# Sliding-window attention with a SwiGLU block: one attention unit takes another place in the source, and some VectorE additions lose their priority

## The chip, the cores and the metric

The kernel runs on 1 core of one Trainium2 chip. The metric is the device time of one execution in microseconds (us). The time before is 343.68 us, the median of 3 runs (343.43 to 343.70).

## The reference

Attention with 8 batches, 8 heads, 576 positions and a head size of 64 is followed by a gated feed-forward block on the 4608 resulting rows of 512 numbers.

```python
scores = scale * np.matmul(q, k.transpose(0, 1, 3, 2))
mask = (rel >= 0) & (rel < 128)                 # rel = query position - key position
scores = np.where(mask, scores - slopes * np.abs(rel), -1e9)
attn = softmax(scores)                           # over the keys
x = np.matmul(attn, v)                           # heads side by side: 4608 x 512
g = x @ w_gate                                   # 512 x 1536
out = (g * sigmoid(g) * (x @ w_val)) @ w_out     # 1536 x 512
```

## The kernel before, in words

**Units and blocks.** Two batches make a group, `s`, of 1152 rows: four tiles of 128 rows from the first batch, four from the second, and one tile that combines the last 64 rows of both. These nine tiles are units `(s, p)`, `p` from 0 to 8, numbered 0 to 35. Unit 8 is the first combined one. The feed-forward part works in 9 blocks of 512 rows. Block 0 takes units 0 to 3, block 1 takes units 4 to 7, and so on; block 8 takes the four combined units. So unit 7 is the last of the four that block 1 needs.

**What a unit does.** TensorE transposes the keys and queries of the first ranks (`transposed`, L218); from rank 11 on a DMA on the sync queue does it (L239). `scores` makes the products of queries and keys in PSUM (`ps`, L278; or `psc`, L313, for tiles with only 128 queries), ScalarE takes the exponential (L284, L317), and VectorE multiplies with a mask (`ex`, L290; `exc`, L321). Unit 8 has three such `exc` tiles of 128x1024 elements, unit 7 has one. `weighted` (L325) makes the attention-value products on TensorE (`av`, L345), and VectorE divides them by the row sum in two halves (reciprocal L347, `x` L348). `x_transposed` (L358) transposes `x` on TensorE (`px`, L371), and ScalarE copies it into `xT` (L375).

**What a block does.** For blocks 0 to 5, each of 12 column groups has a gate product `pg` and a value product `pv` on TensorE, four matmuls of 512 columns each (L397). ScalarE makes a tanh of the gate (L415), VectorE multiplies it with the gate (`uu`, L416) and then with the value product (`hT`, L427). `pg` and `pv` share three PSUM banks (tag `gv`), so a product waits for VectorE to have read the one three before it. Scores, `av`, `px` and transposed tiles share four other banks (tag `a`). Blocks 6 to 8 compute gate and value with Strassen-Winograd's seven products of half size (`gate_val_by_seven`, L612). There a unit of two column groups holds the banks X, Y and Z (`gX`, `gY`, `gZ`); `third` adds Y and a saved sum into `v1` (L661), `seventh` adds X and a saved product into `v2` (L669), and `fourth` then writes X anew (L624), which must wait until that addition has read it. The output projection is `project` for block 0 (`po`, L451) and a seven-product form for all others (`strassen`, L504, products L532); its sums S2, S3 and S4 of the activations are made on VectorE (L485 to L488), and its results leave PSUM through `half_plus` (L535), among others.

**What sets the order.** GpSimd issues its loads in an order written out by hand. TensorE, VectorE and ScalarE keep the order of the source in the first part (up to 8 steps of the feed-forward part). After that a scheduler orders each engine's instructions: of those that it believes ready it takes the one that stands first in the source, and `tc.high_priority()` moves an instruction ahead. From step 60 (block 2) TensorE again keeps the order of the source, and VectorE and ScalarE stay with the scheduler. Before step 60 the scheduler also draws work forward as filler, so the projection of block 0 (`po`, L451) runs between the steps of units 7 and 8. The source interleaves the two parts: `everything` (L939) goes through the steps of `ffn` and after each one takes as many steps of the generator `attention` (L840) as a target says; it counts them in `n_att`. In `attention`, the turn of unit `i` emits the transpositions and scores of unit `i + 1`, then `weighted(i)`, then loads (`loads_to`, `ahead`), then `x_transposed(i)`; from unit 13 on the order differs a little (`late`).

The functions of the change:

Of the kernel before, what the change touches and what calls it, by code (L numbers as in the profile page):

```python
# [31 lines left out]
SEVEN_FROM = 6  # L32
# [19 lines left out]
def kernel(  # L52
# [10 lines left out]
    nc = tc.nc  # L63
# [440 lines left out]
    def strassen(n, t):  # L504

        h = hT[n]
        A11, A12 = h[:, 0:HM, 0:256], h[:, HM:NMB, 0:256]
        S1, A22 = h[:, 0:HM, 256:512], h[:, HM:NMB, 256:512]
        S2, S3, S4 = hsum[n]
        cols = slice(t * P, (t + 1) * P)  # L510
        end = n == NBLK - 1
        seeded = SEVEN_FROM <= n + 1 < NBLK
        factor = 1.0 if n >= SEVEN_FROM else 0.5
        if end:
            X, Y = (ps_a.tile([P, HC], FP32, name="po", tag="a", bufs=4) for _ in range(2))
            p2 = ps_f.tile([P, HC], FP32, name="p2", tag="gv")
        else:
            po = ps_f.tile([P, 2, HC], FP32, name="po", tag="po", bufs=1)
            X, Y = po[:, 0, :], po[:, 1, :]
            p2 = (ps_f.tile([P, HC], FP32, name="p2", tag="gv") if seeded  # L520
                  else ps_a.tile([P, HC], FP32, name="p2", tag="a"))
        top, low = (opool.tile([P, DM], FP32, name="osb", tag="osb") for _ in range(2))
        if end and t:
            spare = [opool.tile([P, DM], FP32, name="osb", tag="osb") for _ in range(2)]
            p1s, p5s, u2s = spare[0][:, 0:HC], spare[0][:, HC:DM], spare[1][:, 0:HC]
        else:
            p1s, p5s, u2s = (supool.tile([P, HC], FP32, name=i, tag=i, bufs=1)
                             for i in ("p1s", "p5s", "u2s"))

        def product(dst, a, b, start=False):  # L530
            for m in range(HM):
                nc.tensor.matmul(dst, a[:, m, cols], b[:, m, :], start=(start and m == 0),  # L532
                                 stop=(m == HM - 1), skip_group_check=True)

        def half_plus(dst, a, b):  # L535
            with tc.high_priority():
                nc.vector.scalar_tensor_tensor(out=dst, in0=a, scalar=factor, in1=b,
                                               op0=ALU.mult, op1=ALU.add)

        product(X, A11, B11, True)  # L540
        if seeded:
            nc.scalar.copy(p2, X)
        else:
            nc.scalar.mul(p1s, X, factor)
        yield
        product(p2, A12, B21, not seeded)
        if seeded:
            nc.vector.tensor_scalar_mul(top[:, 0:HC], p2, factor)
        else:
            half_plus(top[:, 0:HC], p2, p1s)  # L550
        if end and t:
            store(n, t, top, 0, HC)
        yield
        product(X, S2, T2)
        nc.scalar.mul(u2s, X, factor)
        yield
        product(Y, S1, T1, end)
        if end and t:
            nc.vector.tensor_scalar_mul(p5s, Y, factor)
        else:  # L560
            nc.scalar.mul(p5s, Y, factor)
        yield
        product(X, S3, T3)
        half_plus(low[:, HC:DM], X, p5s)
        if end and t:
            store(n, t + 2, low, HC, DM, True)
        yield
        product(Y, S4, B22)
        half_plus(top[:, HC:DM], Y, u2s)
        store(n, t, top, HC if end and t else 0, DM, end)  # L570
        yield
        product(X, A22, T4)
        if end:
            nc.vector.tensor_scalar_mul(low[:, 0:HC], X, factor)
        else:
            nc.scalar.mul(low[:, 0:HC], X, factor)
        store(n, t + 2, low, 0, HC if end and t else DM, end)
        yield
# [33 lines left out]
    def gate_val_by_seven(n):  # L612

        x = xT[n]
        A11, A12 = x[:, 0:HK, 0:256], x[:, HK:NKB, 0:256]
        S1, A22 = x[:, 0:HK, 256:512], x[:, HK:NKB, 256:512]
        S2, S3, S4 = xsum.pop(n)
        hT[n] = hpool.tile([P, NMB, 512], FP16, name="hT", tag="hT")
        live = {}

        def product(dst, w, c0, a, start=False):
            for i in range(2):
                for kb in range(HK):
                    nc.tensor.matmul(dst[:, i, :], w[:, kb, c0 + i * P:c0 + (i + 1) * P], a[:, kb, :],  # L624
                                     start=(start and i == 0 and kb == 0),
                                     stop=(i == 1 and kb == HK - 1), skip_group_check=True)

        def first(u):
            X, Y = (ps_a.tile([P, 2, 256], FP32, name=i, tag="a", bufs=4) for i in ("gX", "gY"))
            Z = ps_f.tile([P, 2, 256], FP32, name="gZ", tag="gv")  # L630
            live[u] = X, Y, Z
            product(X, G1, 2 * u * P, A11, True)
            nc.scalar.copy(Z, X)

        def fifth(u):
            Y = live[u][1]
            product(Y, tsum[u][0], 0, S1, True)
            p5 = epool.tile([P, 2, 256], FP32, name="p5", tag="exc", bufs=5)
            nc.scalar.copy(p5, Y)
            live[u] += (p5,)  # L640

        def second(u):
            Z = live[u][2]
            product(Z, G2, 2 * u * P, A12)
            s = supool.tile([P, 2, 256], FP16, name="s1", tag="tt")
            nc.scalar.activation(s, Z, AF.Silu)
            live[u] += (s,)

        def sixth(u):
            X = live[u][0]  # L650
            product(X, tsum[u][1], 0, S2)
            u2 = epool.tile([P, 2, 256], FP32, name="u2", tag="exc", bufs=5)
            nc.scalar.copy(u2, X)
            live[u] += (u2,)

        def third(u):
            X, Y, Z, p5, u2, s = live[u][:6]
            product(Y, V2, 2 * u * P, S4)
            v_ = supool.tile([P, 2, 256], FP16, name="v1", tag="uu")
            with tc.high_priority():  # L660
                nc.vector.tensor_add(v_, Y, u2)  # L661
            nc.vector.tensor_mul(hT[n][:, 2 * u:2 * u + 2, 0:256], s, v_)

        def seventh(u):
            X, Y, Z, p5, u2, s = live[u]
            product(X, tsum[u][2], 0, S3)
            v_ = supool.tile([P, 2, 256], FP16, name="v2", tag="uu")
            with tc.high_priority():
                nc.vector.tensor_add(v_, X, p5)  # L669
            live[u] += (v_,)  # L670

        def fourth(u):
            X, v_ = live[u][0], live[u][-1]
            del live[u]
            product(X, tsum[u][3], 0, A22)
            s = supool.tile([P, 2, 256], FP16, name="s2", tag="tt")
            nc.scalar.activation(s, X, AF.Silu)  # L677
            nc.vector.tensor_mul(hT[n][:, 2 * u:2 * u + 2, 256:512], s, v_)  # L678

        return {f.__name__: f for f in (first, second, third, fourth, fifth, sixth, seventh)}  # L680

    def seven_steps():
# [105 lines left out]
    def transposes_to(n):  # L788
        nonlocal done_t
        while done_t < n:  # L790
            transpose(done_t)
            done_t += 1
# [7 lines left out]
    def run(steps):  # L800
        for fs in steps:
            for f in fs:
                f()
            yield
# [35 lines left out]
    def attention():  # L840

        waiting = []
        transposes_to(need[FIRST])
        for _ in run(scores(FIRST)):
            yield FIRST
        for i in range(FIRST, last + 1):
            late = i >= LATE
            if i < last:
                transposes_to(need[i + 1])
                for n, _ in enumerate(run(scores(i + 1))):  # L850
                    yield i - len(waiting)
                    if n == 2 and late:
                        weighted(i)
                        yield i - len(waiting)
            if not late or i == last:
                weighted(i)
                yield i
            loads_to(i + 7)
            ahead(i)
            yield i - len(waiting)  # L860
            if late and i < X_DMA_FROM:
                if waiting:
                    x_transposed(waiting.pop(0))
                waiting.append(i)
                yield i
                yield i
                continue
            while waiting:
                x_transposed(waiting.pop(0))
            x_transposed(i)  # L870
            yield i
            yield i + 1
# [135 lines left out]
```

## Time and profile before

| what | value |
|---|---|
| time, median of 3 runs | 343.68 us (343.43 to 343.70) |
| profiled execution: its own time | 343.68 us |
| profiled execution: span of its instructions | 341.9 us |
| TensorE (PE) busy | 329.5 us, 2983 matmuls |
| VectorE (DVE) busy | 277.1 us, 652 instructions |
| ScalarE (ACT) busy | 206.8 us, 412 instructions |
| GpSimd (POOL) busy | 109.8 us, 136 instructions |
| clock granted to TensorE | 1.00 in each of the stages shown below |
| DMA | 37.37 MB, mean 109 GB/s |

All times inside the profile are microseconds from the start of the span. A line of the timeline has a start, a duration, the engine, the source line, the operation, what it writes and reads by the program's names, and how many of its kind follow each other. In brackets stands how long the engine was idle before it and what ended that. A line of the table by stages has, for each engine, its busy time in the stretch and the number of its instructions, then the granted clock, the DMA share and the DMA rate. A matmul's duration includes its way through the array, so consecutive ones overlap; the distance from start to start is what one costs.

### The profile page before, as it was taken

What the parts mean: (1) busy time and instruction counts of PE and PEld (TensorE: products, weight loads), DVE (VectorE), ACT (ScalarE), POOL (GpSimd) and SP (SyncE); (2) the same over time, 40 slices, a digit from 0 to 9 for tenths busy, and PEclk for the clock granted to TensorE, in tenths of its full rate; (3) what the DMA queues carried; (4) which work ended last, traced back from release to release, by engine and by line L of the source; (5) the groups of instructions that cost most, each with busy time, mean ns of one, the idle gap of its engine ahead of it and who ended that gap; (6) DMA issues with size and microseconds to landing.
All of it is one profiled execution on the core that took longest, in us unless ns stands there. A gap on an engine that the chain in (4) does not pass through costs nothing.

```text
span 341.9 us, 7784 instructions
## 1 busy us (share of the span) xinstructions
PE 329.5 (96%) x2983; PEld 218.4 (64%) x2983; DVE 277.1 (81%) x652; ACT 206.8 (60%) x412; POOL 109.8 (32%) x136
## 2 busy tenths in 40 slices
PE   7999989999999999999999999999999999999995
PEld 3484445444456565566665655666688888888884
DVE  5577885999798769998899999999855975775683
ACT  3758676465765666566665647563467666676640
POOL 8967682549856165924008000000000000000000
PEclk9999999999999999999999999999999999999999
DMA  9999999799999999999949942031101101011024
GB/s 149 168 180 176 163 165 159 71 144 153 160 172 149 170 159 174 177 144 148 197 109 81 160 63 87 15 63 47 63 2 61 60 3 64 10 55 63 0 71 116
DMA packets 160037, 37.37 MB, mean 109 GB/s; under 512 B 147328, under 2 KB 155648, under 8 KB 160000
## 3 DMA queue, kind: packets, MB, share of 16 engines
q0 software_dynamic: 118336, 18.62, 82.8%
q1 hardware_dynamic: 40976, 17.64, 27.9%
q10 hardware_dynamic: 688, 0.62, 0.6%
q8 instruction: 23, 0.38, 0.5%
q14 instruction: 14, 0.11, 0.1%
HBM read 37.91 MB, written 9.44 MB: 138 GB/s over the span
## 4 chain that ended last, share of the span: by engine, by line
PE 75%; DVE 13%; DMA 4%; ACT 4%; issue 2%; POOL 0%; SPq 0%; DVEq 0%; ACTq 0%
PE po L532 16%; PE pg L397 14%; PE pv L397 14%; PE gX L624 8%; PE gY L624 4%; PE av L345 4%; PE ps L278 3%; DMA qn<-in_q_dram 3%; PE p L532 2%; PE po L451 2%; PE gZ L624 2%; DVE hT L427 2%; ACT ex L284 2%; DVE uu L416 1%; DMA stage<-in_q_dram 1%
## 5 line engine op out<-in xcount | busy, mean ns | idle before, releaser
L397 PE MATMUL pv<-xT,wv_sb 128*128 128x512 f16 (+2 forms) x320 | 76.5, 358 | 0.3 <-DVE hT L427 0.2
L397 PE MATMUL pg<-xT,wg_sb 128*128 128x512 f16 (+2 forms) x320 | 75.8, 358 | 0.3 <-DVE xT L373 0.2
L415 ACT ACTIVATE tt<-pg 128x512 f16<-128x512 f32 (+2 forms) x70 | 41.3, 590 | 47.6 <-PE pg L397 46.5
L284 ACT ACTIVATE ex<-ps 128x512 f16<-128x512 f32 x96 | 50.0, 605 | 9.9 <-PE ps L278 9.9
L416 DVE SCALAR_TENSOR_TENSOR uu<-tt,pg 128x512 f16<-128x512 f16 (+2 forms) x69 | 45.9, 666 | 11.3 <-ACT tt L415 11.0
L427 DVE TENSOR_TENSOR hT<-uu,pv 128x512 f16<-128x512 f16 (+2 forms) x70 | 46.6, 666 | 3.0 <-PE pv L397 1.3
L185 POOL DMA_DIRECT2D va<-in_v_dram x40 | 34.4, 863 | 37.3 <-PE av L345 30.6
L532 PEld LDWEIGHTS <-hT 128*128 128x128 f16 x384 | 36.9, 98 | 11.3 <-issue 1.7
L397 PEld LDWEIGHTS <-wv_sb 128*128 128x128 f16 x320 | 28.3, 98 | 24.5 <-issue 2.6
L397 PEld LDWEIGHTS <-wg_sb 128*128 128x128 f16 x320 | 28.3, 98 | 22.9 <-issue 2.0
L191 POOL DMA_DIRECT2D kn<-in_k_dram x39 | 33.3, 858 | 20.7 <-DMA kT<-kn 11.4
L191 POOL DMA_DIRECT2D qn<-in_q_dram x39 | 33.5, 864 | 15.3 <-DMA va<-in_v_dram 9.8
L532 PEld LDWEIGHTS <-S 128*128 128x128 f16 x288 | 27.2, 98 | 9.9 <-DVE S L487 2.2
L290 DVE TENSOR_TENSOR ex<-ex,m_reg 128x1024 f16<-128x1024 f16 x42 | 28.8, 686 | 3.0 <-ACT ex L284 2.9
L348 DVE TENSOR_TENSOR x<-av,rec 128x256 f16<-128x256 f32 x72 | 28.7, 419 | 0.4
L532 PE MATMUL po<-T,S 128*128 128x256 f16 x192 | 26.8, 273 | 1.2 <-DVE S L487 0.9
L532 PE MATMUL po<-T,hT 128*128 128x256 f16 x192 | 26.0, 273 | 0.1
L678 DVE TENSOR_TENSOR hT<-s,v 128x512 f16<-128x512 f16 x18 | 7.6, 424 | 18.4 <-ACT s L677 18.4
L317 ACT ACTIVATE exc<-psc 128x512 f16<-128x512 f32 x40 | 21.3, 607 | 1.9 <-PE psc L313 1.9
L345 PEld LDWEIGHTS <-ex 128*128 128x128 f16 x384 | 17.4, 97 | 4.6 <-issue 1.1
L345 PE MATMUL av<-va,ex 128*128 128x65 f16 x384 | 19.3, 193 | 0.7 <-ACT ex L284 0.7
L278 PE MATMUL ps<-qT,kT 64*128 64x256 f16 x192 | 16.7, 272 | 0.4 <-DVE qT L223 0.2
(134 smaller groups left out, 536.0 us busy)
## 6 DMA issues: line engine op xcount, KB each, us to landing
out_dram<-osb SPq DMA_DIRECT2D x32, 256.0 KB, 2.6
va<-in_v_dram POOLq DMA_DIRECT2D x32, 128.0 KB, 8.1
qn<-in_q_dram POOLq DMA_DIRECT2D x31, 128.0 KB, 7.8
kn<-in_k_dram POOLq DMA_DIRECT2D x31, 128.0 KB, 8.6
wg_sb<-in_moe_w_gate_dram POOLq DMA_DIRECT2D x6, 256.0 KB, 7.8
wv_sb<-in_moe_w_val_dram POOLq DMA_DIRECT2D x6, 256.0 KB, 7.9
wo_sb<-in_moe_w_out_dram POOLq DMA_DIRECT2D x2, 768.0 KB, 9.2
kn<-in_k_dram POOLq DMA_DIRECT2D x8, 64.0 KB, 7.7
```

The costliest lines, as they stand in the source:

```text
L185: nc.gpsimd.dma_start(va[rank][p0:p1, :, 0:D], src)
L191: nc.gpsimd.dma_start(t_[p0:p1], src)
L284: nc.scalar.activation(e[:, o:o + 2, :], banks[q4][par], AF.Exp, scale=scale)
L290: nc.vector.tensor_mul(e[:, o, :], e[:, o, :], reg[:, o, :])
L345: nc.tensor.matmul(av[:, j, :], w, val, start=(n == 0), stop=(n == len(todo) - 1))
L348: nc.vector.tensor_mul(x[:, 4 * half:4 * half + 4, :], av[:, :, 0:D], rec.broadcast_to([P, 4, D]))
L397: nc.tensor.matmul(ps[:, c0:c1], w[:, kb, ms], xT[n][:, kb, c0:c1], start=(kb == 0 and c0 == 0), stop=(kb == NKB - 1 and c1 == 512), skip_ ...
L415: nc.scalar.activation(tt, pg[:, c0:c1], AF.Tanh, scale=0.5)
L416: nc.vector.scalar_tensor_tensor(out=uu, in0=tt, scalar=one if (n, m) == PIN else 1.0, in1=pg[:, c0:c1], op0=ALU.add, op1=ALU.mult)
L427: nc.vector.tensor_mul(hT[n][:, m, c0:c1], acted[(n, m)][1][:, c0:c1], pv[:, c0:c1])
L532: nc.tensor.matmul(dst, a[:, m, cols], b[:, m, :], start=(start and m == 0), stop=(m == HM - 1), skip_group_check=True)
L624: nc.tensor.matmul(dst[:, i, :], w[:, kb, c0 + i * P:c0 + (i + 1) * P], a[:, kb, :], start=(start and i == 0 and kb == 0), stop=(i == 1 an ...
```

## The change

Two things are changed.

In `attention`, the turn of unit 7 gets an order of its own: `weighted(7)` and `x_transposed(7)` come first, then the transpositions and scores of unit 8 (the first combined one), then the loads. The turn yields 9 times and no longer 10, and it reports unit 7 as done before the scores of unit 8.

In the last blocks, VectorE's additions lose `tc.high_priority()`: `v1` in `third` and `v2` in `seventh` (blocks 6 to 8), and those in `half_plus` for the projections of blocks 5 to 8.

```diff
@@ -533,7 +533,7 @@
         def half_plus(dst, a, b):
-            with tc.high_priority():
+            with tc.high_priority() if n + 1 < SEVEN_FROM else ExitStack():
                 nc.vector.scalar_tensor_tensor(out=dst, in0=a, scalar=factor, in1=b,
                                                op0=ALU.mult, op1=ALU.add)
 
@@ -657,16 +657,14 @@
             X, Y, Z, p5, u2, s = live[u][:6]
             product(Y, V2, 2 * u * P, S4)
             v_ = supool.tile([P, 2, 256], FP16, name="v1", tag="uu")
-            with tc.high_priority():
-                nc.vector.tensor_add(v_, Y, u2)
+            nc.vector.tensor_add(v_, Y, u2)
             nc.vector.tensor_mul(hT[n][:, 2 * u:2 * u + 2, 0:256], s, v_)
 
         def seventh(u):
             X, Y, Z, p5, u2, s = live[u]
             product(X, tsum[u][2], 0, S3)
             v_ = supool.tile([P, 2, 256], FP16, name="v2", tag="uu")
-            with tc.high_priority():
-                nc.vector.tensor_add(v_, X, p5)
+            nc.vector.tensor_add(v_, X, p5)
             live[u] += (v_,)
 
@@ -845,6 +843,18 @@
             yield FIRST
         for i in range(FIRST, last + 1):
             late = i >= LATE
+            if i == 7:
+                weighted(i)
+                yield i
+                x_transposed(i)
+                yield i + 1
+                transposes_to(need[i + 1])
+                for _ in run(scores(i + 1)):
+                    yield i + 1
+                loads_to(i + 7)
+                ahead(i)
+                yield i + 1
+                continue
             if i < last:
                 transposes_to(need[i + 1])
                 for n, _ in enumerate(run(scores(i + 1))):
```

## The prediction

> **What bounds the kernel now.** I read the shares of busy time first, then the table by stages, then the timelines of the stages that the change touches. The profiled execution took 343.68 us, which is the median too, with a span of 341.9; 1.78 us lie around the span. So every sum below is taken from 343.68.
>
> ```profile
> PE 329.5 (96%) x2983; PEld 218.4 (64%) x2983; DVE 277.1 (81%) x652; ACT 206.8 (60%) x412; POOL 109.8 (32%) x136
> ```
>
> The stages, for one core (busy time of PE, weight loads, DVE, ACT, POOL; clock; DMA):
>
> ```profile
> 48.50:57.00 8.50, 7.49 (x89) 4.52 (x86) 6.51 (x17) 6.25 (x13) 2.94 (x4) 1.00 1.88 173
> 57.00:69.50 12.50, 12.48 (x85) 5.53 (x83) 10.77 (x22) 5.97 (x11) 5.91 (x7) 1.00 1.29 97
> 69.50:97.00 27.50, 26.52 (x216) 12.74 (x214) 25.09 (x60) 17.77 (x34) 20.11 (x25) 1.00 2.24 152
> 97.00:170.00 73.00, 71.74 (x682) 43.99 (x679) 62.65 (x142) 45.09 (x92) 33.90 (x40) 1.00 1.89 167
> 170.00:240.00 70.00, 69.96 (x618) 41.84 (x615) 69.09 (x172) 39.19 (x79) 7.61 (x10) 1.00 0.69 78
> 240.00:342.00 102.00, 96.78 (x866) 84.14 (x864) 68.34 (x156) 61.57 (x122) 0.00 (x0) 1.00 0.14 48
> ```
>
> TensorE sets the end: it is idle for 12.4 us of 341.9 (341.9 minus 329.5), and 5.2 of that lie after 240, most of it behind the last matmul. From start to start in the timelines a matmul costs 0.216 us at 512 columns, 0.109 at 256, 0.056 at 128 and 0.029 at 65; the 64-row score products run in pairs (0.056 a pair of `psc`). At these distances TensorE's work is the same before and after, since no matmul is added. So only waits of TensorE can be won or lost. VectorE is close behind: 69.09 of 70 us from 170 to 240, 25.09 of 27.5 from 69.5 to 97.
>
> One page speaks against this reading. The Trainium skill ("TensorE: Matmul & The Clock Gate", "Back-to-back issue gap") gives about 131 ns as the sustained distance at 512 columns; the trace has four in 0.86 us, so 215 ns, and I go by the trace. By the page's figure the seven moved projection matmuls below would cost 0.92 and not 1.51 us, and the first gain would be 1.45 and not 0.86.
>
> **Part B, unit 7 first.** The stretch before block 1 can start (first `pg` at 56.69) has the largest waits after the opening:
>
> ```profile
> 49.46 0.28 PE L371 MATMUL px<-idm,x 128*128 128x128 f16 x2 [0.57 <-DVE x L348]
> ...
> 51.35 0.38 PE L313 MATMUL psc<-qT,kT 64*128 64x128 f16 x7 [0.20 <-ACT xT L375]
> ...
> 55.74 0.27 PE L371 MATMUL px<-idm,x 128*128 128x128 f16 x2
> ...
> 56.69 0.59 PE L397 MATMUL pg<-xT,wg_sb 128*128 128x512 f16 x2
> ```
>
> Block 1 waits for unit 7's `px` (55.74), which stands behind 24 score products, behind `av`, and behind VectorE's mask multiplications. In the built program of the changed kernel, TensorE goes after the last `pv` of block 0 (48.51): `px` of unit 6, `av` of unit 7, four projection matmuls, `px` of unit 7 among eight transpositions, one more projection matmul, then block 1. I walk through it with the durations of these rows. The mask multiplication for unit 7 still ends at 50.00, so `av` ends at 50.6; VectorE finishes `hT` at 50.94 (0.68, 0.34 behind the second half of unit 6's `x`), so the projection starts at 51.0 and covers the two reciprocals and two halves of `x` (50.87 to 51.85); `px` ends at 52.3, ScalarE's copy (0.59) at 52.93, and block 1 starts at 52.98. That is 3.71 us earlier, with 7 projection matmuls (1.51), 24 score products (0.67) and 12 transpositions (0.67) still to do: **gain 0.86**.
>
> What comes due next is VectorE. Its three mask multiplications (0.69 each) now lie between the evictions of block 1, where each pair of products takes TensorE 1.72 us and VectorE two times 0.60. Before, VectorE stood idle there:
>
> ```profile
> 52.32 0.69 DVE L321 TENSOR_TENSOR exc<-exc,m_c 128x1024 f16<-128x1024 f16 x1 [1.06 <-ACT exc L317]
> ...
> 58.38 0.75 DVE L416 SCALAR_TENSOR_TENSOR uu<-tt,one,pg 128x512 f16<-128x512 f16 x1 [1.64 <-ACT tt L415]
> ```
>
> In the new order its queue is unbroken from 54.7 to 68.1: I add 0.60 per eviction or mask multiplication, 0.67 per weight sum of L475, 0.34 per short one. TensorE then waits 0.3 for a `gv` bank before the fourth `pg` of block 1, 0.3 before its `pv`, and 0.7 for `x` of unit 8; this gives back 0.4. At 73 `av` waits 0.6 for the second mask multiplication of unit 10, which gives back 0.15 more. But VectorE has by then done one weight sum more than before, so the waits before `px` of unit 10 (0.24 idle at 85.96, 0.1 at 84.2) go, gain 0.5, and 0.1 more follows up to 95. The waits at 94.5 to 95.7 (0.46 and 0.20, `av` behind four full banks) stay. At 97 TensorE is **0.9 ahead**; the ends are 0.3, the lead at 75, and 1.3, if the small waits of 75 to 87 (0.4 in sum, not named here) go as well.
>
> The loads don't stop this. Unit 7's values and the first half of the projection weights have landed by 42.4 and 49.3. GpSimd's queue keeps its order; on the sync queue one key transposition passes one output store, which nobody waits for. The keys and queries of the next group arrive at the pace of the transfers: the queries of unit 11 land at 76.3 and are used at 77.9, 77.4 after the change.
>
> Because the turn has one yield less, all later attention steps stand one slot earlier against the feed-forward steps, 0.7 to 0.9 us of TensorE's work; the order differs up to 226 us. Of the larger waits there, the one at 107.74 (0.42 from start to start, beyond the matmul's own 0.216) goes, since an `av` now fills it; the one at 119.87 (0.69 idle) stays with the same neighbours; the one at 142.47 (0.48) goes, but in its place the scores of unit 20 come only 0.7 us behind a `px` whose bank ScalarE must clear first, behind a tanh: 0.45. A second product after 101 finds its bank 0.35 later. Three more products stand 0.86 instead of 1.1 to 1.3 us behind what ScalarE must copy first; the same distance cost 0.42 at 107.74 and nothing in two later places. **Net 0** (0.42 and 0.48 against 0.45 and 0.35). The bounds are a gain of 0.9, if the two new waits don't come, and a loss of 1.2, if each of those three products waits 0.42.
>
> **Part A, the priorities.** In the built program VectorE's order after 240 differs in only two places, where one block's units follow the next block's. The first:
>
> ```profile
> 276.22 0.68 DVE L661 TENSOR_TENSOR v<-gY,u 128x512 f16<-128x512 f32 x1
> 276.81 0.42 DVE L487 TENSOR_TENSOR S<-hT 128x512 f16<-128x512 f16 x1
> 277.15 0.68 DVE L669 TENSOR_TENSOR v<-gX,p 128x512 f16<-128x512 f32 x1
> ```
>
> ```profile
> 277.29 0.39 PE L532 MATMUL po<-T,S 128*128 128x256 f16 x2 [0.54 <-DVE S L487]
> ...
> 278.39 0.60 PE L624 MATMUL gX<-xT,kT 128*128 128x256 f16 x4
> ```
>
> The sum S2 stands behind `v1` (0.59 from start to start), and TensorE goes on at 277.29. After the change S2 goes first and ends at 276.64, so TensorE goes on at 276.70, 0.59 earlier. But `v2` now stands behind S2, `v1` (0.60), S4 (0.33) and the product of L662 (0.34): it runs from 277.82 to 278.50. TensorE comes to the next `gX`, which overwrites what `v2` reads, at 277.79, and may start only at 278.56, against 278.39 before. **A wait takes the place of the one removed, and 0.17 is lost.** The second place (304) has the same order: S2 wins 0.25, `v2` ends at 306.27 and not at 305.60, and `gX` starts at 306.33 and not at 306.16. Together **0.35 lost**. The bounds are a gain of 0.85 (0.59 and 0.25, if `gX` did not wait) and a loss of 0.7 (each place twice as late).
>
> **The sum.** 343.68 - 0.9 + 0 + 0.35 = 343.1; I forecast **343.2**, since a walk by hand leaves out small waits.
>
> **The rivals.** *All of part B arrives, and part A is harmless.* VectorE's lead at 68 (one weight sum and 1.1 us) stays whole: 1.3 at 97, 0.4 from the waits at 107 and 142, nothing lost at 276 and 304: 342.0. For it speak 10.35 us of idle VectorE between 97 and 170, so a lead is not eaten there; against it the two places that I could follow line by line. *VectorE becomes the bound in block 1* (the slower end). Between 57 and 69.5 it was busy 10.77 of 12.5; the three multiplications add 2.07, which is more than the 1.73 left. If each of seven evictions from the third pair on holds its bank 0.2 longer than in my walk, 1.4 more is lost, the 0.9 becomes a loss of 0.5, and with part A 344.5 comes out. It decides from the point where the third gate product of block 1 no longer finds its bank free; the seventh `pg` (69.40) then starts no earlier than before. *The priorities do nothing that can be measured* is the change not doing what it says: 342.8, part of my forecast's own spread.
>
> **Chances.** A measurement of this kernel can tell about 0.2% (0.69 us) from no change. My forecast, within 0.2% (343.0 to 344.4): 0.42. The faster rival and its neighbours below 343.0: 0.38. The slower one above 344.4: 0.20. The range goes from 341.8, the faster rival with 0.2 to spare, to 345.0, the slower one with half of the 1.2 from the slots behind 97; that leaves about 2 in 10 outside. The likeliest case alone lies between 342.9 and 343.9.
>
> **What would show it.** Right: the first `pg` of block 1 at about 53.0; VectorE without a gap from 54.7 to 68; the `gX` after S2 waiting for `v` L669 at two places after 270, and hardly a wait for S L487. Wrong: `px` of unit 7 still waiting beyond 52.5, waits of `pg` and `pv` for `uu` and `hT` of over 1.5 us in sum between 54 and 70, or a new wait of over 0.5 us between 97 and 226.

## The result, and the profile after

The changed kernel is **slower**: 344.54 us, the median of 6 runs (344.50 to 345.03), against 343.68 for the kernel before. The ratio is 1.0029, with a 95% interval of 1.0016 to 1.0042, so about 0.86 us are lost. The forecast was 343.2; the time lies inside the range that was given (341.8 to 345.0), but on the other side of no change, and just above 344.4, where the case "within 0.2%" ends (the slower case had a chance of 0.20). The profiled execution took 344.59 us, with a span of 342.8.

The busy times of the engines hardly change (profile page of the changed kernel, first part):

```profile
PE 329.4 (96%) x2983; PEld 218.7 (64%) x2983; DVE 276.9 (81%) x652; ACT 207.7 (61%) x412; POOL 109.6 (32%) x136
```

The stages do (changed kernel; columns as before: stretch, its length, busy time of PE, weight loads, DVE, ACT and POOL, clock, DMA share, GB/s):

```profile
48.50:57.00 8.50, 7.40 (x78) 3.94 (x77) 5.99 (x17) 4.74 (x10) 2.80 (x4) 1.00 1.88 174
57.00:69.50 12.50, 12.09 (x96) 6.08 (x95) 12.50 (x26) 7.87 (x16) 5.26 (x6) 1.00 1.30 97
69.50:97.00 27.50, 26.59 (x215) 12.93 (x213) 24.34 (x58) 17.33 (x33) 17.79 (x22) 1.00 2.12 138
97.00:170.00 73.00, 71.82 (x680) 44.01 (x678) 62.28 (x143) 46.10 (x93) 36.81 (x44) 1.00 1.99 155
170.00:240.00 70.00, 68.88 (x609) 41.21 (x608) 68.48 (x169) 38.67 (x77) 7.60 (x10) 1.00 0.76 96
```

VectorE is now busy 12.50 of 12.50 us from 57 to 69.5 (10.77 before): its queue has no gap there, as forecast. And from 170 to 240, where nothing in the source was moved, TensorE is busy 68.88 of 70 us and not 69.96. That is where the time went.

**The accounting.** Busy shares show this poorly, so I took the distance from each matmul's start to the next one's, and subtracted what that matmul costs (0.2155 us at 512 columns, 0.109 at 256, 0.056 at 128, 0.029 at 65, and half of it for the score products, which run in pairs). What remains is time that TensorE lost. Part of it is regular (0.10 to 0.15 us nearly wherever score products begin or end), so the differences between kernels are what counts. In us by stretch:

| kernel | 48-66 | 66-97 | 97-139 | 139-147 | 147-195 | 195-203 | 203-246 | 246-310 | elsewhere | sum |
|---|---|---|---|---|---|---|---|---|---|---|
| before | 3.48 | 3.54 | 2.80 | 0.74 | 2.40 | 0.25 | 1.57 | 1.06 | 10.63 | 26.5 |
| changed | 2.93 | 3.47 | 2.71 | 1.33 | 1.96 | 1.39 | 1.89 | 1.39 | 10.49 | 27.6 |
| difference | -0.55 | -0.07 | -0.09 | +0.59 | -0.44 | +1.14 | +0.32 | +0.33 | -0.14 | +1.1 |

The last matmul ends 1.07 us later (338.79 against 337.72), which is the sum; the span grows by 0.92, since the last stores land 0.15 sooner behind it. The -0.14 "elsewhere" lies in the opening and comes and goes between kernels whose opening is the same (9.76 to 10.07 in the runs below).

So the head gained 0.62 up to 97 us, the priorities cost 0.33, and **1.52 were lost between 97 and 246**, for which the prediction had put zero. The two largest places there, in the changed kernel's timeline of all engines (weight loads and issues left out):

```profile
197.38 0.42 DVE L537 SCALAR_TENSOR_TENSOR osb<-p,p1s 128x256 f32<-128x256 f32 x1
...
197.48 0.63 PE L278 MATMUL ps<-qT,kT 64*128 64x256 f16 x5
...
197.80 0.66 DVE L427 TENSOR_TENSOR hT<-uu,pv 128x512 f16<-128x512 f16 x1
...
198.37 0.42 DVE L348 TENSOR_TENSOR x<-av,rec 128x256 f16<-128x256 f32 x1
...
198.85 0.39 PE L278 MATMUL ps<-qT,kT 64*128 64x256 f16 x3 [0.74 <-DVE x L348]
```

The eight score products of a unit write four banks of the pool `a`. The sixth, the first into the fourth bank, waits until VectorE has read the old content, an `av`, with the second `x`. That instruction stands behind an `osb` and an `hT` in a queue that is full. In the kernel before, the same products were reached later and the `x` was done sooner:

```profile
197.77 0.76 DVE L348 TENSOR_TENSOR x<-av,rec 128x256 f16<-128x256 f32 x2
...
198.10 1.03 PE L397 MATMUL pg<-xT,wg_sb 128*128 128x512 f16 x4
...
199.06 0.61 PE L278 MATMUL ps<-qT,kT 64*128 64x256 f16 x8
```

There a gate product of 0.86 us lies between the projection and the scores, `x` ends at 198.53, and all eight run without a stop. One slot earlier means: without that gate product. The same happens at 217 with a bank that `osb` has still to read (changed kernel):

```profile
216.96 0.45 PE L313 MATMUL psc<-qT,kT 64*128 64x128 f16 x9
...
217.28 0.42 DVE L537 SCALAR_TENSOR_TENSOR osb<-p,p1s 128x256 f32<-128x256 f32 x1
...
217.76 0.38 PE L313 MATMUL psc<-qT,kT 64*128 64x128 f16 x7 [0.35 <-DVE osb L537]
```

At 142 the scores of unit 20 wait first for ScalarE's `xT`, as forecast, but then twice more for the `x` on VectorE (142.18 to 142.94), behind a mask multiplication: 1.05 in three waits (0.30, 0.47 and 0.28), where the kernel before lost 0.48 to S2.

```profile
142.18 0.76 DVE L348 TENSOR_TENSOR x<-av,rec 128x256 f16<-128x256 f32 x2
...
142.66 0.71 PE L278 MATMUL ps<-qT,kT 64*128 64x256 f16 x4 [0.26 <-DVE x L348]
```

### The profile page after: what moved, and what is told of

It is laid out like the page before. It is cut to its first block, busy times and chain, and to the rows that moved or that the text cites. A ratio compares the mean times of both kernels' runs of the same rounds, so it can differ in the third digit from the quotient of the medians.

```text
span 342.8 us, 7785 instructions
## 1 busy us (share of the span) xinstructions
PE 329.4 (96%) x2983; PEld 218.7 (64%) x2983; DVE 276.9 (81%) x652; ACT 207.7 (61%) x412; POOL 109.6 (32%) x136
## 4 chain that ended last, share of the span: by engine, by line
PE 60%; DVE 26%; ACT 6%; issue 4%; DMA 2%; ACTq 0%; SPq 0%; DVEq 0%
PE po L532 14%; PE pg L397 10%; PE pv L397 10%; PE gX L624 8%; DVE uu L416 5%; DVE hT L427 5%; PE gY L624 4%; PE av L345 3%; DVE ex L290 2%; ACT ex L284 2%; PE po L451 2%; PE ps L278 2%; PE p L532 2%; DVE x L348 2%; PE gZ L624 2%
## 5 line engine op out<-in xcount | busy, mean ns | idle before, releaser
L397 PEld LDWEIGHTS <-wg_sb 128*128 128x128 f16 x320 | 29.0, 98 | 24.2 <-issue 1.9
L290 DVE TENSOR_TENSOR ex<-ex,m_reg 128x1024 f16<-128x1024 f16 x42 | 28.5, 686 | 3.9 <-ACT ex L284 3.7
```

The lines of the kernel that those rows point to most:

```text
L290: nc.vector.tensor_mul(e[:, o, :], e[:, o, :], reg[:, o, :])
L397: nc.tensor.matmul(ps[:, c0:c1], w[:, kb, ms], xT[n][:, kb, c0:c1], start=(kb == 0 and c0 == 0), stop=(kb == NKB - 1 and c1 == 512), skip_ ...
```

## The experiments

The head is here the stretch up to 97 us, and the seams are the two places of part A, at 276 and 304 us, where the units of one block follow those of the next. My theory T after this result: the one-slot shift of the attention steps loses the time, at single places where TensorE comes too early for a bank that VectorE has still to read. Rival R1: the head leaves VectorE with a backlog that costs later, and the slots are innocent. Rival R2: the priorities cost more than was forecast.

**The tenth step put back** (head and priorities as changed, slots as before from 66 us on).

```diff
                 ahead(i)
                 yield i + 1
+                yield i + 1
                 continue
```

> The changed kernel with a tenth step in the turn of unit 7, so that from TensorE's instruction 576 (about 66 us) on its order is again that of the kernel before; the head and the priorities stay changed. Theory T (the one-slot shift of the attention steps loses the time between 97 and 230 us, the head gains 0.6 to 0.8, the priorities lose 0.33): 343.68 - 0.6 + 0.33 = 343.4, between 343.2 and 343.6, and TensorE's lead of 0.6 to 0.8 at 97 us is still there at 230. Rival R1 (VectorE leaves the head with another backlog, and that is what costs later, whatever the slots are): 344.3 to 344.6 as in the changed kernel, with the lead lost between 140 and 230. Rival R2 (the priorities cost all of it): 344.3 or more, with a lead of 0.6 to 0.8 at 240 that is lost after it.

Measured: 343.54 us, ratio 1.000 (0.9992 to 1.0009). The loss between 97 and 246 is gone: that stretch is as in the kernel before (table below). R1 and R2 fall, since head and priorities are both in this kernel. But one part of T fell too: TensorE's lead at 97 is 0.24 (3.15 + 3.63 lost from 48 to 97, against 7.02) and not 0.6. With ten steps TensorE waits at places where the changed kernel doesn't: 0.23 at 61.6 for `hT`, in the full VectorE queue of block 1, and 0.24 at 71.1, behind ScalarE's copy of a key tile, as in the kernel before.

**The priorities alone** (the kernel before, with the three priorities taken away as in the change).

```diff
...
-            with tc.high_priority():
-                nc.vector.tensor_add(v_, Y, u2)
+            nc.vector.tensor_add(v_, Y, u2)
...
-            with tc.high_priority():
-                nc.vector.tensor_add(v_, X, p5)
+            nc.vector.tensor_add(v_, X, p5)
```

> The kernel before with the priorities removed and nothing else; only VectorE's order at the two seams (276 and 304 us) differs. My theory: 0.17 lost at each seam, 344.0 (343.9 to 344.1), with gX waiting for v L669 (L667 in this kernel) 0.7 us at the first seam and 0.4 at the second. Rival R2: 344.5, the whole loss. Rival R3 (the sum S2 goes earlier, and gX does not matter): 342.9 to 343.2.

Measured: 343.86, ratio 1.0015 (1.0003 to 1.0027), which is 0.30 above the 343.56 of the kernel before in the same series and 0.04 below the expected range. The waits are the forecast ones (0.76 and 0.42 at `gX`, from start to start beyond the matmul's own cost). R2 and R3 fall.

**Unit 7's turn alone** (the changed kernel with all priorities restored).

> The changed kernel with the priorities put back: unit 7's turn alone. Theory T: 344.54 - 0.33 = 344.2 (344.1 to 344.4), slower than before although the head is earlier. R2 (priorities are all of the loss): 343.7 or less. If the two parts add up, the differences of this kernel and of the one with the priorities alone make the 0.86 of the change.

Measured: 344.53 (344.06 to 344.88), ratio 1.0028 (1.0018 to 1.0039), 0.97 above the kernel before and not the 0.53 that 0.86 less the forecast 0.33 leaves. It misses the expectation by 0.13. Its profiled execution has one wait that the changed kernel's lacks, for a transposition of queries that landed at 87.88 and not at 86.75 (it had started at 80.94 and not at 80.27):

```profile
88.02 0.39 PE L278 MATMUL ps<-qT,kT 64*128 64x256 f16 x4 [0.31 <-DMA qT<-qn]
```

That is 0.47 from start to start. Without it the stretches behave as in the changed kernel (1.32, 1.94, 1.37 and 1.87 lost from 139 to 246) and the seams as before (1.06). How often this wait occurs in the unprofiled runs was not measured, so the additivity of the two parts is shown by the stretches, not by this median.

**The slot alone** (the kernel before, with one step less in unit 7's turn and nothing moved).

```diff
             x_transposed(i)
-            yield i
+            if i != 7:
+                yield i
             yield i + 1
```

> The kernel before with one step less in the turn of unit 7, and nothing moved: the head up to about 66 us is as before, and all later attention steps stand one slot earlier, in the order of the changed kernel from TensorE's instruction 716 (about 81 us) on. Theory T: 1.5 to 1.7 lost between 97 and 240 without the head's gain, 345.2 to 345.4, with ps at about 198 us waiting 0.7 to 1.0 for x L348 of VectorE. Rival R1 (the head's VectorE order is the cause, slots are free): 343.5 to 343.8.

Measured: 345.05, ratio 1.0048 (1.0034 to 1.0063): **1.49 lost by one `yield`**. The sixth score product waits for `x` again, 0.70 at 198.7 (start to start, beyond its own cost), `psc` 0.53 at 217.8, and the three waits at 143 are there. R1 falls for good as the cause: the head is untouched here. But the time is 0.15 below the range of T, and not all of it lies where T put it: 1.11 is lost between 97 and 246, and 0.33 before that, between 66 and 97. So of the 1.52 that the changed kernel lost behind 97, 0.41 is not the slot alone; 0.37 of that is at 198, where the changed kernel comes with the head's lead and waits 0.95 and not 0.70, so part of the lead goes there.

**v1 without priority, v2 with it** (the kernel before otherwise).

```diff
-            with tc.high_priority():
-                nc.vector.tensor_add(v_, Y, u2)
+            nc.vector.tensor_add(v_, Y, u2)
```

> The kernel before, in which only v1 loses its priority; v2 and half_plus keep theirs. VectorE then takes the sum S2 ahead of v1 at the two seams, and v2 still early. Theory (S2's wait was worth 0.5 at the first seam and 0.25 at the second, and gX is held by v2 alone): the wait for S L487 goes, v2 follows v1 at once, and gX starts without a wait: 0.5 to 0.75 less than before, 342.8 to 343.1 against 343.56. Rival (v1 in its later place holds gX as well, or v2 falls behind S4 and the product all the same): 343.9, as with all priorities removed.

Measured: 342.84, ratio 0.9978 (0.9969 to 0.9987). **Part A turned into a gain.** Its timeline at the first seam:

```profile
275.99 0.41 DVE L487 TENSOR_TENSOR S<-hT 128x512 f16<-128x512 f16 x1
276.32 0.68 DVE L660 TENSOR_TENSOR v<-gY,u 128x512 f16<-128x512 f32 x1
...
276.92 0.68 DVE L668 TENSOR_TENSOR v<-gX,p 128x512 f16<-128x512 f32 x1
277.13 0.60 PE L624 MATMUL gX<-m_reg,kT 128*128 128x256 f16 x4
...
277.66 0.60 PE L624 MATMUL gX<-xT,kT 128*128 128x256 f16 x4
```

and that of the changed kernel:

```profile
276.97 0.41 DVE L487 TENSOR_TENSOR S<-hT 128x512 f16<-128x512 f16 x1
277.30 0.68 DVE L660 TENSOR_TENSOR v<-gY,u 128x512 f16<-128x512 f32 x1
...
277.90 0.41 DVE L488 TENSOR_TENSOR S<-hT,S 128x512 f16<-128x512 f16 x1
278.11 0.60 PE L624 MATMUL gX<-m_reg,kT 128*128 128x256 f16 x4
278.23 0.42 DVE L661 TENSOR_TENSOR hT<-s,v 128x512 f16<-128x512 f16 x1
...
278.57 0.68 DVE L667 TENSOR_TENSOR v<-gX,p 128x512 f16<-128x512 f32 x1
...
279.31 0.60 PE L624 MATMUL gX<-xT,kT 128*128 128x256 f16 x4 [0.60 <-DVE v L667]
```

In both, S2 is early. In the first, `v2` follows `v1` at once (0.60 behind it), and `gX` hardly waits (0.53 from start to start of the two groups, against 0.44 for four matmuls); in the second, S4 and a product go between, and `gX` waits. The two seams lose 0.30 in all there, 1.06 before and 1.39 after the change. `half_plus` plays no part that the traces show: with all three priorities taken away ("priorities alone"), only S2 and `v2` stand at other places in VectorE's order (by name, behind 10 us), and here only S2.

**The step put back later.** Two kernels like the changed one, with the missing step given back in a later turn, so that the slots are shifted only up to about 137 us (unit 19, the diff) or 161 us (unit 23 in its place).

```diff
                 waiting.append(i)
+                if i == 19:
+                    yield i
                 yield i
                 yield i
                 continue
```

> The changed kernel with the missing step given back at unit 19, so that the attention steps stand one slot earlier up to about 137 us only, and from there on TensorE's order is that of the kernel before. Priorities stay removed. Theory T (the loss lies at single places behind 141, above all at 142, 198 and 217 us): the lead of 0.7 at 137 stays to 240, 0.3 is lost at the seams: 343.56 - 0.7 + 0.3 = 343.2 (343.0 to 343.4). Rival (any change of slots costs, whatever its place, or the lead is eaten by VectorE): 344.0 to 344.5.

> The same, with the step given back at unit 23 (about 161 us). Theory T: the waits of ps at 142 us (0.6 net) are there, those at 198 and 217 us are not: 343.56 - 0.1 + 0.3 = 343.8 (343.6 to 344.0). If the three steps 343.2, 343.8 and 344.4 (given back at 137, at 161, not at all) come out, the loss sits at these places and not in the slots as such. Rival: the same time as with the step given back at 137, or as without it.

Measured: 343.04, ratio 0.9984 (0.9975 to 0.9993), and 343.87, ratio 1.0008 (0.9999 to 1.0017). Against the kernel before in the same series these are -0.50, +0.33 and, for no step back, +0.86, the three steps of T: a shift up to 137 us costs nothing, one that passes 142 costs 0.8 more, one that passes 198 and 217 another 0.5. The loss sits at places, not in the slots as such. The sizes of the steps are less sure: each median is uncertain by about 0.3 against the kernel before, and by lost time from 97 to 246 (table below) the two steps are 0.7 and 1.0.

**Less work on VectorE.** The changed kernel without the `ex` mask multiplications (L290) from unit 22 on; this leaves out part of the attention's mask, so only its time is read.

```diff
         def mul(q4):
-            if early_tile:
+            if early_tile or i >= 22:
                 return
```

> The changed kernel, in which the mask multiplications of VectorE (128x1024, 0.6 us each from start to start) are left out from unit 22 on, 18 of them, so that VectorE has gaps between 155 and 235 us; TensorE's order is that of the changed kernel. Theory (the banks that ps waits for at 198 us and psc at 217 us are held by reads of x and osb that stand in VectorE's full queue): these waits shrink from 1.0 and 0.5 to less than 0.3 in sum, 344.4 - 1.3 = 343.1 (342.8 to 343.4). Rival (the banks come late because of the order alone, with VectorE idle or not): 344.1 to 344.4.

Measured: 343.42, against 343.54 for the kernel before in its series (ratio 0.9999, 0.9990 to 1.0008), so about 1.0 below the changed kernel, and 0.02 outside the expectation. TensorE's order is the same everywhere and VectorE's from 193.5 to 199 (before that, the scheduler moves some of its instructions forward). But VectorE is busy 5.03 of 7 us from 186 to 193, and 7.00 of 7 in the changed kernel, so it comes earlier to what stands there, and `x` begins as the scores begin:

```profile
197.35 0.92 PE L278 MATMUL ps<-qT,kT 64*128 64x256 f16 x8
197.40 0.42 DVE L348 TENSOR_TENSOR x<-av,rec 128x256 f16<-128x256 f32 x1
```

The eight products run almost through: the wait of 0.95 has shrunk to 0.24, and the 0.54 at 217 to 0.14, in sum 0.38 where less than 0.3 was expected; a wait at 227 (0.14) became one of 0.26 at 226. The waits at 142, ahead of the first mask that was left out, stayed. So it is the full VectorE queue that holds the banks at 198 and 217. For the waits at 142 this was not tested; that they come with the slot is shown by the step given back at 137 and at 161.

**The parts that pay, together**: the head, the step back at unit 19, `v1` without priority, `v2` with it.

> Unit 7's turn as in the change, the step given back at unit 19, v1 without priority, v2 and half_plus with it. If head, slots and seams add up: 0.8 from the head and the slots up to 137 us and 0.7 from the seams, 343.55 - 1.5 = 342.05 (341.9 to 342.3), faster than both kernels. If the seams' gain is lost when TensorE comes earlier: 342.7.

Measured: **341.83**, ratio 0.9947 (0.9930 to 0.9965), 0.07 below the expected range. It is faster than the kernel before by 1.6 us (343.45 in its series) and than the changed kernel by 2.7 (medians of two series).

The lost time of all of them, in us, by the same accounting, to be read beside the rows "before" and "changed" of the first table:

| kernel | 48-66 | 66-97 | 97-139 | 139-147 | 147-195 | 195-203 | 203-246 | 246-310 |
|---|---|---|---|---|---|---|---|---|
| tenth step back | 3.15 | 3.63 | 2.80 | 0.74 | 2.39 | 0.25 | 1.55 | 1.38 |
| priorities alone | 3.78 | 3.54 | 2.80 | 0.74 | 2.39 | 0.25 | 1.54 | 1.37 |
| unit 7 alone | 2.93 | 3.83 | 2.71 | 1.32 | 1.94 | 1.37 | 1.87 | 1.06 |
| slot alone | 3.47 | 3.87 | 2.71 | 1.32 | 1.95 | 1.02 | 1.87 | 1.07 |
| v1 alone | 3.47 | 3.54 | 2.80 | 0.74 | 2.41 | 0.25 | 1.57 | 0.30 |
| back at 137 | 2.93 | 3.47 | 2.70 | 0.64 | 2.41 | 0.25 | 1.58 | 1.40 |
| back at 161 | 2.94 | 3.47 | 2.71 | 1.33 | 2.40 | 0.25 | 1.57 | 1.42 |
| fewer masks | 2.93 | 3.47 | 2.72 | 1.32 | 1.90 | 0.55 | 1.62 | 1.39 |
| all that pays | 2.93 | 3.47 | 2.70 | 0.64 | 2.40 | 0.25 | 1.57 | 0.29 |

The reader is to see that a number changes only where its cause is present, and repeats to a few hundredths otherwise. The 3.78 of the second kernel is a wait of 0.30 for a load of queries at 54.9; the 0.36 extra in "unit 7 alone" is the transposition above.

## Why the prediction was wrong, point by point

**What bounds the kernel: right.** TensorE's busy time is the same to 0.1 us (329.4 against 329.5), and every change of time is a wait of TensorE won or lost. But the 12.4 us of idle time that the prediction takes from the busy shares are too little: by the starts, TensorE lost 26.5 us in the kernel before, and 4.2 us follow its last matmul.

**The head up to block 1: right.** The timeline of TensorE alone in the changed kernel:

```profile
49.29 0.28 PE L371 MATMUL px<-idm,x 128*128 128x128 f16 x2 [0.57 <-DVE x L348]
...
50.82 1.04 PE L451 MATMUL po<-wo_sb,hT 128*128 128x512 f16 x4 [0.22 <-DVE hT L427]
51.69 0.28 PE L371 MATMUL px<-idm,x 128*128 128x128 f16 x2
...
52.81 1.02 PE L397 MATMUL pg<-xT,wg_sb 128*128 128x512 f16 x4
```

The projection starts at 50.82 (51.0 forecast) and block 1 at 52.81 (52.98 forecast); all of this execution is 0.17 early from the opening on, so these are the forecast times. The four projection matmuls take 0.87 from start to start, 217 ns each. No run here shows the 131 ns that the Trainium skill ("TensorE: Matmul & The Clock Gate", "Back-to-back issue gap") states as the sustained distance at 512 columns.

**VectorE's full queue in block 1: right in kind.** Its timeline has no gap over 0.1 from 54.50 to 69, where it stood idle before; the mask multiplications lie between the evictions:

```profile
54.50 0.75 DVE L416 SCALAR_TENSOR_TENSOR uu<-tt,one,pg 128x512 f16<-128x512 f16 x1 [1.51 <-ACT tt L415]
...
57.86 0.69 DVE L321 TENSOR_TENSOR exc<-exc,m_c 128x1024 f16<-128x1024 f16 x1
...
59.06 0.69 DVE L321 TENSOR_TENSOR exc<-exc,m_c 128x1024 f16<-128x1024 f16 x1
```

TensorE lost 0.11 and 0.34 to it at 58.9 and 59.8, and 0.40 at 67.2 (0.3, 0.3 and 0.7 forecast). The rival in which VectorE becomes the bound of block 1 did not happen: 0.55 less is lost from 48 to 66. By the sign that the prediction gave it the margin is small: the seventh `pg` starts at 69.12 and not at 69.40, and 0.17 of that is the earlier opening.

**From 69 to 97: too high.** The waits before `px` of unit 10 were to go, for a gain of 0.5. One of 0.43 went, but 0.27 at 87.0 and 0.19 at 91.4 came, both for `x`; the lead at 97 was 0.62 and not 0.9.

**The slots behind 97: here it failed.** The step is "Net 0", for "all later attention steps stand one slot earlier". It measured a loss of 1.52, more than the bound of 1.2; the slot alone, without the head's lead, lost 1.11 there. The working was right about what it looked at: the wait at 107 went, that at 100 came (0.25; 0.35 forecast), ScalarE's `xT` held the scores at 142 (0.30; 0.45 forecast). What it left out is the other engine that frees banks: it asked only what ScalarE "must copy first", at distances up to 1.3 us of TensorE's work. A score product also needs four banks of which VectorE reads some, and the table by stages, shown in the prediction itself, had VectorE busy 69.09 of 70 us there. An engine with a full queue gives a bank back when its turn comes, and 0.86 us of TensorE's work less in front of such a product can then turn into a wait: 1.14 at 198, 0.32 from 203 to 246, 0.59 around 142. The Trainium skill ("Perfetto Trace Analysis", "Optimizing Tensor Performance", on matmuls) advises rotating independent matmul groups through different banks, so that one group's evacuation overlaps the next one's products. Here four banks rotate, and the row at 198.85 shows 0.74 us of idle TensorE all the same: the rotation hid the evacuation here only where VectorE kept up (0.24 of that product's 0.95 was left with fewer masks). The shift also gained what I had not counted: 0.44 between 147 and 195, of it 0.38 from two waits (173.5 and 181.9) that are no longer there. Its own sign was given: "a new wait of over 0.5 us between 97 and 226" was to show it wrong, and the sixth `ps`, at 198.85, is that wait.

**The priorities: right.** 0.17 was forecast at each seam, and TensorE is 0.16 and 0.17 later there; `gX` waits for `v2` 0.76 and 0.43, S2's waits are gone but for 0.10. The kernels with one part each show it from both sides (+0.30 without any priority, -0.70 with `v2`'s and `half_plus`'s kept).

**The rivals.** The faster one needed all of the lead and harmless seams; neither came. The slower one gave nearly the measured time, 344.5, for a wrong reason: its place was block 1, and the loss lies 130 us later.

## What to carry to other kernels

When a change takes one step out of an interleaving, walk every later product and ask who reads the bank that it writes, on each engine, not only on the one whose waits show now; a bank whose reader stands in a saturated queue comes free at that queue's pace, and work removed in front of the product can then turn into a wait (0.86 us of it less cost 0.70 at 198 in the kernel with the slot alone). If an early shift pays only up to some point, give the slot back before the first bad place: here one `yield` at the right turn was worth 1.5 us. And when a priority is removed to let something else through, look which of the instructions that lost it is awaited soonest by the bounding engine, and keep that one early: of `v1` and `v2` only `v1` could be late.

## What the runs showed of the hardware

The arrival of loads is not the same in every execution: the transposed queries that `ps` needs at 87 landed at 86.75 in the changed kernel and at 87.88 in "unit 7 alone", which has the same order up to there. The loads in front had been issued about 1.1 us later (kn at 75.77 against 74.66 on GpSimd), and the wait cost 0.47, where the head had won 0.62. Why they were issued later was not measured. Where no load is involved, the lost time repeats from kernel to kernel to about 0.05 us, although the mean clock granted to TensorE lay between 0.997 and 1.0 in the profiled executions.
